# The third batch's q and v are loaded during the second pass of an attention and MLP kernel

## The chip, the cores and the metric

The kernel runs on one core of a Trainium2 chip. The metric is device time in microseconds of one execution of the whole program. The program before takes 803.91 us, the median of nine runs from 802.67 to 804.8. A profiled execution gives the trace that all views below come from.

## The reference

Attention with grouped heads over 8 batches of 384 positions, 16 query heads, 4 key and value heads, head size 64; then a ResMLP block over the 1024 columns that the heads make together:

```python
scores = (q @ k^T) / sqrt(64)                  # each k, v head serves 4 q heads
x      = softmax(scores) @ v                   # 8 x 384 x 1024
u      = x + lam * (w_tok @ (alpha1 * x + beta1))
out    = u + lam * (relu((alpha2 * u + beta2) @ w_ch1) @ w_ch2)   # 1024 -> 4096 -> 1024
```

Inputs and output are float32; the kernel computes its matrix products from bf16 operands.

## The kernel before

**Passes.** After an opening part that computes the attention of the first batch, `main(b)` runs once for each of the 8 batches. A pass has two stages on the tensor engine (TensorE, PE). The *W1 stage* computes `h = relu(a2 @ w_ch1)` in 16 chunks of 256 hidden columns (L414): a chunk is two groups of 8 matmuls 128x384. The *W2 stage* computes `h @ w_ch2` in 6 output tiles of 32 matmuls 128x512 (L447). `w_ch2` stays in SBUF from the first pass on; `w_ch1` does not fit beside it and is loaded anew in each pass, chunk by chunk.

**Attention of the next batch rides along.** `main` yields at points of both stages, four times in each chunk of the W1 stage (units 0 to 63), and the loop at the end of the kernel calls there what a table has for that unit. `side(b + 1)` gives two tables, one for each stage. In the W2 stage of pass b go scores, exp, products with v and token mixing of batch b + 1. In the W1 stage go only its preparations: for the second pass, `turns` in `side(2)` has `q_transpose` at units 16, 24 and 32, six 128x128 transposes on TensorE into a PSUM bank each (L203), and a copy to `qT` by DVE (L205). Each handles two of the eight head pairs; so pairs 2 to 7 of the third batch are turned in chunks 4, 6 and 8.

**Batches and passes.** The index of a batch counts from 0. "Third batch" is b = 2, and its attention is prepared in the second pass (b = 1).

**Loads of weights and inputs.** POOL issues the loads that cast from float32 to bf16, and they all go through one queue in the order of the program: W1 chunks (`load_w1`, L134), w2 (`load_w2`, L139), q (`load_q`, L116, four loads of four heads, 192 KB each) and v (`load_v`, L111, three of 64 KB). W1 has a ring of RING = 5 buffers. In `main`, after chunk c, `load_w1` issues the load of the chunk five further on; the issue waits on POOL until chunk c has been read, and whatever stands behind it on POOL waits with it. At the end of the W1 stage of the first pass POOL issues the first five chunks of the second pass and then calls `load_next(2)`: `place_k` (four copies of k on POOL), q and v of the third batch.

**SP.** SP issues k's loads (L96), the stores of the output (L454) and DMA transposes: a2 for the next pass (L297), k (`flip_k`, L119) and, where the table `moves` says so, q (`flip_q`, L123). For b == 1, `moves` has `flip_k` and `flip_q` for pairs 0 and 1 of the third batch, at unit 1 of the W1 stage. SP's instructions run in order; behind those two come the k loads for the fourth batch.

From the third pass on, q of the next batch is loaded and flipped by DMA during W2 stages; the change does not touch this.

Of the kernel before, what the change touches and what calls it, by code (L numbers as in the profile page):

```python
# [12 lines left out]
def kernel(  # L13
# [23 lines left out]
    bf = mybir.dt.bfloat16  # L37
# [6 lines left out]
    B, Hq, S, D = q.shape  # L44
    Hkv = k.shape[1]
    G = Hq // Hkv
    DM = Hq * D
    DFF = moe_w_ch1.shape[1]
    P = 128
    NST = S // P  # L50
# [6 lines left out]
    NCH = NNT // CW  # L57
    RING = 5
# [5 lines left out]
    sb = ST(tc.tile_pool(name="sb", bufs=2))  # L64
# [22 lines left out]
    def by_st(ap):  # L87
        return ap.rearrange("h (p st) d -> p st h d", st=NST)

    ks, k2s, qrs = {}, {}, {}  # L90
# [8 lines left out]
    def place_k(b, i, hs=(0, 1)):  # L99
        if b not in k2s:  # L100
            k2s[b] = sb.tile([P, NST, Hkv, 2, D], bf, tag="k2", name="k2", bufs=1)
        copies = [nc.gpsimd.tensor_copy] * 2
        if b == 1 or b == 0 == i:
            copies = (nc.vector.tensor_copy, nc.vector.tensor_copy if i else nc.scalar.copy)
        lo, hi = hs[0], hs[-1] + 1
        for a in range(2):
            copies[a](out=k2s[b][:, :, 2 * i + lo:2 * i + hi, a, :], in_=ks[b][i][:, lo:hi].rearrange("p h st d -> p st h d"))

    def load_v(b, sts=range(NST)):
        for st in sts:  # L110
            nc.gpsimd.dma_start(out=vt[b % 2][:, st, :, :D], in_=by_st(v[b])[:, st])  # L111

    def load_q(b):
        qrs[b] = sb.tile([P, Hq, NST, D], bf, tag="q_raw", name="q_raw", bufs=1)
        for h in range(0, Hq, G):
            nc.gpsimd.dma_start(out=qrs[b][:, h:h + G], in_=q[b, h:h + G].rearrange("h (p st) d -> p h st d", st=NST))  # L116

    def flip_k(b):
# [11 lines left out]
    def load_w1(n):  # L130
        if n < B * NCH:
            t = sb.tile([P, NDT, CW * P], bf, tag="w1", name="w1", bufs=RING)
            c = n % NCH
            nc.gpsimd.dma_start(out=t, in_=w1src[:, :, c * CW * P:(c + 1) * CW * P])  # L134
            w1_tiles[n] = t

    def load_w2(dw, i, n):
        r, cs = slice(i * NNT // n, (i + 1) * NNT // n), slice(dw * 512, (dw + 1) * 512)
        nc.gpsimd.dma_start(out=w2[:, r, cs], in_=w2src[:, r, cs])  # L139

    def bank(shape, tag, name, dtype=f32):
        if tag == "three":
            return threes[0].tile(shape, dtype, tag="sc", name=name, bufs=3)
        if tag == "mm":
            return mms.tile(shape, dtype, tag="mm", name=name, bufs=2)
        return psum.tile(shape, dtype, tag=tag, name=name, bufs=2 if tag == "sc" else 1)
# [9 lines left out]
    def evac(eng):  # L156
        return nc.scalar.copy if eng == "ACT" else nc.vector.tensor_copy
# [16 lines left out]
    def side(b):  # L174
# [177 lines left out]
        if not first:  # L352


            turns = {16 + 8 * i: [(q_transpose, 2 + 2 * i, 2, "three")] for i in range(3)} if b == 2 else {}
            if b == 1:
                turns = {4: [(split, 2, 4, 0)], 8: [(split, 2, 4, 1)], 12: [(k_transpose, 0)],
                         16: [(q_transpose, 0, 2, "av")], 20: [(k_transpose, 2)]}
                for i in range(3):
                    turns[24 + 4 * i] = [(q_transpose, 2 + 2 * i, 2, "av")]  # L360
                for i in range(4):
                    turns[34 + 4 * i] = [(spread, (2 * i, 2 * i + 1), (1, 3), "tp", "ACT")]
                for i in range(2):
                    turns[50 + 4 * i] = [(spread, range(4 * i, 4 * i + 4), (3, 4), "av", "ACT")]
            return turns, {
                0: [(scores3, 0)], 4: [(av, 0)], 6: [(scores3, 1)], 8: [(tok_flip, 0)], 11: [(av, 1)],
                13: [(scores3, 2, True)], 15: [(av, 2)], 16: [(tok_flip, 1)], 18: [(tok_flip, 2)], 19: [(av, 3)],
                21: [(scores3, 3)], 23: [(tok_flip, 3)], 25: [(av, 4)], 27: [(scores3, 4)], 29: [(tok_flip, 4)],
                31: [(av, 5)], 33: [(scores3, 5, True)], 35: [(av, 6), (tok_flip, 5)], 37: [(av, 7)],
                39: [(tok_flip, 6)], 41: [(tok_flip, 7)]}  # L370
# [25 lines left out]
    def load_next(b):  # L396
        place_k(b, 0)
        place_k(b, 1)
        load_q(b)
        load_v(b)  # L400


    def main(b):
        a2T = a2Ts[b % 2]
        x = xs.pop(b)
        n = S + 1 if b == 0 else S
        for c in range(NCH):
            w1 = w1_tiles.pop(b * NCH + c)
            for j in range(CW):
                nt = c * CW + j  # L410
                begun = b == 0 and nt in early
                ps = early[nt] if begun else bank([P, 512], "mm", "h")
                for dt in range(0 if begun else NDT):
                    nc.tensor.matmul(out=ps[:, :n], lhsT=w1[:, dt, j * P:(j + 1) * P],  # L414
                                     rhs=a2T[:, dt, :n], start=(dt == 0), stop=(dt == NDT - 1))
                    if dt == 3:
                        yield 0
                c1 = bias1[:, nt:nt + 1]
                if b == 0:
                    evac("DVE" if nt % 2 else "ACT")(out=c1, in_=ps[:, S:n])  # L420
                if nt % 2 == 0:
                    nc.scalar.activation(out=hT[:, nt, :], in_=ps[:, :S], func=RELU, bias=c1)  # L422
                else:
                    nc.vector.tensor_scalar(out=hT[:, nt, :], in0=ps[:, :S], scalar1=c1,  # L424
                                            scalar2=0.0, op0=ADD, op1=mybir.AluOpType.max)
                yield 0

            if b or c + RING < NCH:
                load_w1(b * NCH + c + RING)
            if b == 0 and c == NCH - RING:  # L430
                for i in range(3, 8):
                    load_w2(0, i, 8)
                for i in range(8):
                    load_w2(1, i, 8)
            if b == 0 and c == NCH - 1:
                for i in range(RING):
                    load_w1(NCH + i)
                load_next(2)
        for dw in range(NDW):
            cs = slice(dw * 512, (dw + 1) * 512)  # L440
            for ms in range(NST):
                ps = bank([P, 512], "mm", "ch")
                o = sb.tile([P, 512], f32, tag="tmp", name="o", bufs=4)
                last = (b, dw, ms) == (B - 1, NDW - 1, NST - 1)
                for lo, hi in ((0, 256), (256, 384), (384, 512)) if last else ((0, 512),):
                    for nt in range(NNT):
                        nc.tensor.matmul(out=ps[:, lo:hi], lhsT=hT[:, nt, ms * P:(ms + 1) * P],  # L447
                                         rhs=w2[:, nt, dw * 512 + lo:dw * 512 + hi], start=(nt == 0), stop=(nt == NNT - 1))
                        if nt % 4 == 3 and nt < NNT - 1:
                            yield 1  # L450
                    c = slice(dw * 512 + lo, dw * 512 + hi)
                    nc.vector.tensor_tensor(out=o[:, lo:hi], in0=ps[:, lo:hi], in1=lam_t[:, c], op=MUL)  # L452
                    nc.vector.tensor_tensor(out=o[:, lo:hi], in0=o[:, lo:hi], in1=x[:, ms, c], op=ADD)  # L453
                    nc.sync.dma_start(out=out[b].rearrange("(p st) d -> p st d", st=NST)[:, ms, c], in_=o[:, lo:hi])  # L454
                yield 1
# [3 lines left out]
    with tc.manual_schedule(engines=order):  # L459
# [110 lines left out]
        load_k(2)  # L570
        for b in range(B):
            us = side(b + 1) if b + 1 < B else ({}, {})
            moves = [(0, 1, flip_k, 2), (0, 1, flip_q, 2, 0, 2)] if b == 1 else []
            if 0 < b < B - 2:
                moves += [(1, 1, load_k, b + 2), (1, 2, load_next, b + 2), (1, 34, flip_k, b + 2), (1, 36, flip_q, b + 2, 0, 2),
                          (1, 37, flip_q, b + 2, 2, 2), (1, 42, flip_q, b + 2, 4, 2), (1, 43, flip_q, b + 2, 6, 2)]
            for i, u, *m in moves:
                us[i].setdefault(u, []).append(m)
            done = [0, 0]
            for second in main(b):  # L580
                if b == second - done[1] - 1 == 0:
                    lead_banks.close()
                    threes.append(ST(tc.psum_pool(name="threes", bufs=3)))
                for f, *a in us[second].get(done[second], []):
                    f(*a)
                done[second] += 1
# [28 lines left out]
```

The softmax here doesn't subtract the row's maximum and nothing guards it: scores larger than these inputs give would overflow.

## Time and profile before

| what | value |
|---|---|
| median of nine runs | 803.91 us |
| profiled execution | 804.8 us, of which span of the trace 803.0 us |
| TensorE busy | 794.8 us, 99% of the span |
| granted clock of TensorE | 0.999 of full |
| second pass, W1 stage | 133.0 to 176.8 us |
| third pass, W1 stage | 232.0 to 273.6 us |
| W1 loads issued on POOL (L134) | 128 of 512 KB, 0.87 us of POOL each |
| W1 loads issued 134 to 180 us, issue to landing | 9.5 / 10.5 / 10.8 us (least, median, most) |
| W1 loads issued 232 to 276 us, issue to landing | 6.3 / 8.2 / 9.5 us |

The page of a profile shows busy time of each engine, the span in 40 slices, the DMA queues, the chain that ended last, and the costliest groups of instructions. Times in the views are in us from the start of the span. In a timeline each line has start, duration, engine, line of the kernel, operation, what is written and read, count, and in brackets how long the engine stood idle before it and who ended that. PEld is TensorE's weight load, which runs beside its matmuls. An idle time of a loading engine such as POOL means that it waited for a buffer, and costs nothing in itself. "Landing" is the time from a DMA's issue to its completion. The DMA share in a table of windows counts the packets' time in all queues against 16 engines, and can exceed 1.

### The profile page before, as it was taken

How to read it: one execution, taken by the hardware profiler on the slowest of the kernel's cores; microseconds unless marked ns; L12 is line 12 of the kernel's file. 1: busy time of each engine (PE TensorE's matmuls, PEld its weight loads, DVE VectorE, ACT ScalarE, POOL GpSimd, SP SyncE). 2: the span in 40 equal slices, each digit the busy share in tenths (PEclk: the TensorE clock that was granted, in tenths of full speed). 3: DMA queues.
4: the chain of work that ended last, by engine and by line, in shares of the span. 5: the costliest groups of instructions: out<-in, count | busy, mean ns of one | idle time of the engine just before them, and what ended most of it. 6: DMA issues, size and time to landing. Idle time of an engine off the chain costs nothing.

```text
span 803.0 us, 14253 instructions
## 1 busy us (share of the span) xinstructions
PE 794.8 (99%) x6141; PEld 453.3 (56%) x6141; DVE 344.2 (43%) x667; ACT 226.5 (28%) x308; POOL 182.0 (23%) x241
## 2 busy tenths in 40 slices
PE   8999999999999999999999999999999999999997
PEld 4766555655556555565555655566555655556545
DVE  7652555225552256323662236622365225552122
ACT  7624331223402233123221233122431223312100
POOL 9234231342013500135002340033300330003000
PEclk9999999999999999999999999999999999999999
DMA  9999999999269962999439991499914994139611
GB/s 189 202 194 202 202 207 160 190 198 134 65 132 187 198 95 62 160 189 196 74 80 156 198 195 45 95 175 198 160 47 113 169 198 86 47 64 179 88 40 40
DMA packets 232575, 112.58 MB, mean 140 GB/s; under 512 B 81976, under 2 KB 226368, under 8 KB 232512
## 3 DMA queue, kind: packets, MB, share of 16 engines
q0 software_dynamic: 170752, 83.47, 78.8%
q1 hardware_dynamic: 61216, 27.81, 14.0%
q8 instruction: 48, 0.79, 0.4%
q10 hardware_dynamic: 544, 0.39, 0.1%
q14 instruction: 15, 0.12, 0.1%
HBM read 170.53 MB, written 12.58 MB: 228 GB/s over the span
## 4 chain that ended last, share of the span: by engine, by line
PE 85%; DMA 9%; issue 3%; DVE 1%; POOL 1%; SPq 0%; ACT 0%; POOLq 0%; DVEq 0%
PE ch L447 37%; PE h L414 36%; DMA w<-in_moe_w_ch_dram 9%; PE sc L217 4%; PE sc L252 3%; PE sc L275 3%; POOL w L134 1%; PE h L168 1%; DMA hT<-in_moe_lam_dram 1%; PE tok L275 0%; PE av L252 0%; PE ut L292 0%; DVE x L258 0%; PE tp L203 0%; DVE hT L532 0%
## 5 line engine op out<-in xcount | busy, mean ns | idle before, releaser
L447 PE MATMUL ch<-w,hT 128*128 128x512 bf16 (+2 forms) x1600 | 357.6, 371 | 0.9 <-DVE o L452 0.9
L414 PE MATMUL h<-a2T,w 128*128 128x384 bf16 (+1 forms) x2016 | 332.1, 326 | 0.6 <-DMA w<-in_moe_w_ch_dram 0.6
L414 PEld LDWEIGHTS <-w 128*128 128x128 bf16 x2016 | 196.2, 98 | 131.2 <-DMA w<-in_moe_w_ch_dram 2.7
L134 POOL DMA_DIRECT2D w<-in_moe_w_ch_dram x128 | 112.2, 877 | 527.8 <-PE h L414 507.5
L447 PEld LDWEIGHTS <-hT 128*128 128x128 bf16 x1600 | 144.7, 98 | 152.6 <-issue 10.1
L226 ACT ACTIVATE es<-sc 128x1024 bf16<-128x1024 f32 x126 | 121.4, 1023 | 187.7 <-PE sc L217 178.8
L424 DVE TENSOR_SCALAR hT<-h,bias 128x384 bf16<-128x384 f32 x128 | 79.1, 618 | 216.0 <-PE h L414 215.4
L422 ACT ACTIVATE hT<-h,bias 128x384 bf16<-128x384 f32 x128 | 74.3, 580 | 305.0 <-PE h L414 304.4
L452 DVE TENSOR_TENSOR o<-ch,vecs 128x512 f32<-128x512 f32 (+2 forms) x50 | 33.5, 669 | 108.8 <-PE ch L447 108.8
L252 PEld LDWEIGHTS <-es 128*128 128x128 bf16 x1008 | 38.2, 97 | 13.2
L275 PEld LDWEIGHTS <-wtokT 128*128 128x128 bf16 x576 | 37.4, 98 | 12.3 <-DVE a L265 1.7
L217 PE MATMUL sc<-qT,kT 64*128 64x384 bf16 (+2 forms) x576 | 41.9, 271 | 0.2
L252 PE MATMUL sc<-v,es 128*128 128x65 bf16 x1008 | 39.8, 193 | 0.0
L257 DVE RECIPROCAL rinv<-sc 128x6 f32<-128x6 f32 x56 | 10.8, 193 | 67.2 <-PE sc L252 66.4
L282 DVE TENSOR_TENSOR x<-sc,x 128x384 f32<-128x384 f32 x56 | 31.0, 553 | 20.0 <-PE sc L275 20.0
L275 PE MATMUL sc<-a,wtokT 128*128 128x128 bf16 x504 | 37.3, 219 | 0.0
L217 PEld LDWEIGHTS <-kT 64*128 64x128 bf16 x576 | 21.7, 94 | 24.0 <-issue 19.0
L453 DVE TENSOR_TENSOR o<-o,x 128x512 f32<-128x512 f32 (+2 forms) x50 | 33.5, 671 | 1.7
L286 DVE TENSOR_TENSOR a<-x,vecs 128x384 bf16<-128x384 f32 x56 | 31.8, 567 | 1.9
L263 DVE TENSOR_TENSOR a1f<-x,vecs 128x384 f32<-128x384 f32 x56 | 31.2, 558 | 1.9
L265 DVE TENSOR_TENSOR a<-a1f,vecs 128x384 bf16<-128x384 f32 x56 | 31.2, 558 | 1.9
L258 DVE TENSOR_TENSOR x<-sc,rinv 128x384 f32<-128x384 f32 x56 | 31.2, 558 | 1.9
(80 smaller groups left out, 212.0 us busy)
## 6 DMA issues: line engine op xcount, KB each, us to landing
w<-in_moe_w_ch_dram POOLq DMA_DIRECT2D x144, 512.0 KB, 9.0
out_dram<-o SPq DMA_DIRECT2D x47, 256.0 KB, 2.1
q_raw<-in_q_dram POOLq DMA_DIRECT2D x28, 192.0 KB, 8.8
kst<-in_k_dram SPq DMA_DIRECT2D x16, 192.0 KB, 6.2
v<-in_v_dram POOLq DMA_DIRECT2D x24, 64.0 KB, 8.7
a2T<-a SPq DMA_TRANSPOSE x56, 2.3
qg<-in_q_dram POOLq DMA_DIRECT2D x3, 192.0 KB, 5.8
stage<-in_q_dram ACTq DMA_DIRECT2D x2, 192.0 KB, 3.7
```

What stands on the lines that cost most here:

```text
L134: nc.gpsimd.dma_start(out=t, in_=w1src[:, :, c * CW * P:(c + 1) * CW * P])
L217: nc.tensor.matmul(out=sc[:, hh, k % 4:k % 4 + n], lhsT=kT[r, sk, 2 * p // G, :], rhs=qT[r, p, st:st + n, :], start=True, stop=True)
L226: nc.scalar.activation(out=e, in_=sc, func=EXP, scale=scale_qk)
L252: nc.tensor.matmul(out=av[:, hh, sq, :], lhsT=ess[k // 4][:, m % 2, k % 4, :], rhs=vb[:, sk, hk, :], start=(sk == 0), stop=(sk == NST - 1))
L275: nc.tensor.matmul(out=ps[:, tt, :], lhsT=wtokT[:, st, tt * P:(tt + 1) * P], rhs=a1s[p][:, st, :], start=(st == 0), stop=(st == NST - 1 an ...
L286: nc.vector.tensor_tensor(out=a2s[p], in0=u, in1=bc(al2, p), op=MUL)
L414: nc.tensor.matmul(out=ps[:, :n], lhsT=w1[:, dt, j * P:(j + 1) * P], rhs=a2T[:, dt, :n], start=(dt == 0), stop=(dt == NDT - 1))
L422: nc.scalar.activation(out=hT[:, nt, :], in_=ps[:, :S], func=RELU, bias=c1)
L424: nc.vector.tensor_scalar(out=hT[:, nt, :], in0=ps[:, :S], scalar1=c1, scalar2=0.0, op0=ADD, op1=mybir.AluOpType.max)
L447: nc.tensor.matmul(out=ps[:, lo:hi], lhsT=hT[:, nt, ms * P:(ms + 1) * P], rhs=w2[:, nt, dw * 512 + lo:dw * 512 + hi], start=(nt == 0), sto ...
L452: nc.vector.tensor_tensor(out=o[:, lo:hi], in0=ps[:, lo:hi], in1=lam_t[:, c], op=MUL)
L453: nc.vector.tensor_tensor(out=o[:, lo:hi], in0=o[:, lo:hi], in1=x[:, ms, c], op=ADD)
```

## The change

For the third batch only: `load_next(2)` at the end of the first pass's W1 stage is replaced by its `place_k` calls. q's four loads are issued one by one in the second pass, after the W1 loads that follow chunks 1, 2, 3 and 4. v's three loads are issued after the W1 load that follows chunk 11. The DMA transpose of pairs 0 and 1 on SP is taken away, and TensorE turns all four groups of q, at units 24, 32, 40 and 48 (chunks 6, 8, 10, 12).

```diff
-    def load_q(b):
-        qrs[b] = sb.tile([P, Hq, NST, D], bf, tag="q_raw", name="q_raw", bufs=1)
-        for h in range(0, Hq, G):
+    def load_q(b, hs=range(0, Hq, G)):
+        if b not in qrs:
+            qrs[b] = sb.tile([P, Hq, NST, D], bf, tag="q_raw", name="q_raw", bufs=1)
+        for h in hs:
             nc.gpsimd.dma_start(out=qrs[b][:, h:h + G], in_=q[b, h:h + G].rearrange("h (p st) d -> p h st d", st=NST))
...
-            turns = {16 + 8 * i: [(q_transpose, 2 + 2 * i, 2, "three")] for i in range(3)} if b == 2 else {}
+            turns = {24 + 8 * i: [(q_transpose, 2 * i, 2, "three")] for i in range(4)} if b == 2 else {}
...
             if b == 0 and c == NCH - 1:
                 for i in range(RING):
                     load_w1(NCH + i)
-                load_next(2)
+                place_k(2, 0)
+                place_k(2, 1)
+            if b == 1 and c in range(1, 5):
+                load_q(2, [G * (c - 1)])
+            if b == 1 and c == NCH - RING:
+                load_v(2)
...
-            moves = [(0, 1, flip_k, 2), (0, 1, flip_q, 2, 0, 2)] if b == 1 else []
+            moves = [(0, 1, flip_k, 2)] if b == 1 else []
```

## The prediction

> **What bounds the kernel now.** I read the page first: TensorE is busy 794.8 of 803.0 us at full granted clock in all 40 slices, so a change can only lose or win where TensorE waits. Then I compared the W1 stage of the second pass (the one that the change touches) with that of the third and fourth, in a table of windows: length of the window, busy time of each engine, and at the end granted clock, DMA share, GB/s.
>
> ```profile
> 133.00:177.00 44.00, 43.40 (x276) 25.66 (x275) 12.34 (x21) 9.28 (x16) 13.12 (x15) 1.00 1.32 180
> 232.00:273.60 41.60, 41.60 (x257) 25.05 (x256) 10.65 (x17) 9.30 (x16) 13.12 (x15) 1.00 1.34 189
> 328.64:370.25 41.61, 41.61 (x257) 24.96 (x256) 10.65 (x17) 9.28 (x16) 13.12 (x15) 1.00 1.33 188
> ```
>
> An undisturbed W1 stage lasts 41.6 us, 2.60 a chunk. The second pass's lasts from 133.02 to 176.8, 43.8. Of the 2.2 us more, three turns of q on TensorE are 3 x 0.34 = 1.0 (the third batch's pairs 2 to 7), and 1.2 is waiting for W1. The timeline of weight loads shows where:
>
> ```profile
> 149.33 0.44 PEld L414 LDWEIGHTS <-w 128*128 128x128 bf16 x4 [0.60 <-DMA w<-in_moe_w_ch_dram]
> ...
> 163.56 2.39 PEld L414 LDWEIGHTS <-w 128*128 128x128 bf16 x16 [0.77 <-DMA w<-in_moe_w_ch_dram]
> 166.25 2.39 PEld L414 LDWEIGHTS <-w 128*128 128x128 bf16 x16 [0.30 <-DMA w<-in_moe_w_ch_dram]
> 168.88 2.39 PEld L414 LDWEIGHTS <-w 128*128 128x128 bf16 x16 [0.25 <-DMA w<-in_moe_w_ch_dram]
> 171.52 2.39 PEld L414 LDWEIGHTS <-w 128*128 128x128 bf16 x16 [0.24 <-DMA w<-in_moe_w_ch_dram]
> 174.17 2.39 PEld L414 LDWEIGHTS <-w 128*128 128x128 bf16 x16 [0.27 <-DMA w<-in_moe_w_ch_dram]
> ```
>
> From chunk 11 on each chunk starts 2.64 us after the last, at the pace of its load and not of its 16 matmuls. So the end of this stage is set by the DMA queue. The windows around it say when that queue had room:
>
> ```profile
> 125.00:132.00 7.00, 7.00 (x48) 3.71 (x46) 4.05 (x8) 0.00 (x0) 0.00 (x0) 1.00 1.62 185
> 132.00:136.00 4.00, 4.00 (x25) 2.25 (x24) 1.57 (x3) 0.58 (x1) 0.00 (x0) 1.00 0.19 59
> 136.00:144.00 8.00, 8.00 (x51) 4.83 (x50) 2.05 (x4) 1.74 (x3) 2.75 (x4) 1.00 1.24 136
> 144.00:177.00 33.00, 32.40 (x209) 19.01 (x208) 8.72 (x16) 6.96 (x12) 10.37 (x12) 1.00 1.44 201
> ```
>
> Full until 132, nearly empty to 136, disturbed to 144 (136 GB/s), then full at about 198 GB/s to the end of the stage. The POOL timeline says whose loads these are:
>
> ```profile
> 99.84 0.88 POOL L134 DMA_DIRECT2D w<-in_moe_w_ch_dram x1 [2.99 <-DVE a L265]
> 100.71 2.19 POOL L107 CAST k<-kst 128x384 bf16<-128x384 f32 x4
> 102.86 0.76 POOL L116 DMA_DIRECT2D q_raw<-in_q_dram  x1
> ...
> 122.80 0.74 POOL L111 DMA_DIRECT2D v<-in_v_dram  x1 [3.38 <-DMA w<-in_moe_w_ch_dram]
> 136.08 0.88 POOL L134 DMA_DIRECT2D w<-in_moe_w_ch_dram  x1 [12.54 <-PE h L414]
> ```
>
> The list of DMA issues, cut to one issue at a time, gives landings. Chunk 4, issued at 99.84, lands at 125.1. The third batch's q lands behind it at 126.5, 127.3, 128.4 and 130.2, its v by 131.5. Chunk 5 can be issued only at 136.08, when chunk 0 gives up its buffer. So today q and v travel while nobody waits for the queue.
>
> **The change, part by part.**
>
> *q and v leave 102.9 to 131.5.* Gain: nothing. They are behind chunks 0 to 4 in the same queue, so those land no earlier; the matmuls from 78 to 133 show no wait; chunk 0 starts at 133.02 because the W2 stage ends then. The hole in the queue grows from 4 to about 11 us and stays unused, since chunk 5 still needs chunk 0's buffer.
>
> *q, four loads of 192 KB, behind chunks 6, 7, 8 and 9.* On POOL each issue takes 0.74 us, beside 0.87 for W1, in a period of 2.6: no cost. In the queue, consecutive q loads of a later batch land at 188.5, 189.4, 190.4, 191.4: 1.05 us each once they follow one another. All four lie ahead of chunk 10 in a queue that sets the stage's end: 4 x 1.05 = +4.2 us. What could hide it is the hole at 132 to 136, but they are issued from about 139.6 on. The rows alone would allow a smaller cost only if q ran in gaps, and from 144 on there are none (201 GB/s).
>
> *One DMA transpose of q gone from SP (pairs 0 and 1, issued at 136.67 behind k's).* This is the disputed term. Below: its data phase when nothing else runs, seen in the fine DMA rows at 224 to 232, is 0.93 us (196 KB at about 211 GB/s). Above: from 136 to 144 the queues moved 136 GB/s where 198 would do, which is 8 x 62 = 0.5 MB or 2.5 us lost, and with its own 1.0 that is 3.5 if all of the loss were its doing; part of it is not, as the first chunk of the third and fourth pass starts slowly too. Nearest row: landings counted from the first packet of the first chunk issued in the stage. In the third pass (no transposes then) the second and third chunk land 8.7 and 11.3 us after it; in the second pass, from 138.2, 11.1 and 13.7. The difference is 2.4; the second pass carries in that time also the two k loads (2 x 192 KB, about 2 us), which in the third lie ahead of the first packet, but which will now move at 138 to 140, while the first chunk runs slowly in any case. I leave 0.5 for them: -1.9 us. The two k loads on SP, queued behind the transpose, go out 1.6 us earlier and cost the same bytes.
>
> The Trainium skill, "Advanced Engine Details and Errata", X-Bar Transpose (TRN2), says that transposing DMAs are as fast as plain ones. Alone this one is, in the trace; beside W1 its packets are spread over 139.9 to 144.6, with 1 us at 141.5 in which hardly anything moves. By the rule the term would be its bytes, -1.0, and the sum +3.2. "DMA: Bandwidth & Descriptors", Specifications, wants 512 B per transfer for full rate; a q row in SBUF has 384 B. The trace has q at 188 GB/s against 198 for W1, so the loss is 5% here, and it is in the 1.05.
>
> *Four turns of q on TensorE instead of three, at chunks 6, 8, 10, 12 instead of 4, 6, 8.* One more turn is 0.34 us of TensorE and a DVE copy of 0.56; DVE is busy 12.3 of 44 us. On a stage paced by loads the turn lies inside the waits. A turn needs its q: the first, 0.65 us into chunk 6 (149.3), with q landing near 148.5, has 0.8 us to spare. If q were later, chunk 7's weights are behind it in the same queue, so this wait replaces one that would come anyway.
>
> *v behind chunk 11's issue.* Its queue place is behind the next pass's chunk 0, which lands near 179; three loads of 0.5 us land by 181. The first product with v comes 5.3 us into the W2 stage (182.1 now, 184.6 then). Cost nothing, 3 us of cover. Its 1.5 us of queue delay only chunks of the third pass, which have 50 us.
>
> **The sum, walked chunk by chunk.** New landing = old landing - 1.9 + 1.05 for each q load ahead. Old landings of chunks 6 to 15: 149.3, 151.9, 154.6, 157.2, 159.9, 163.5, 166.2, 168.9, 171.5, 174.2. New: 147.4, 151.0, 154.8, 158.5, 162.2, 165.9, 168.5, 171.2, 173.8, 176.5. TensorE takes 2.60 a chunk, 2.94 with a turn, and starts at the later of its own end and the landing: chunk 6 at 148.6, then 151.6, 154.8, 158.5, 162.2, 165.9, 168.5, 171.4, 174.0, 176.6, end 179.2. Against 176.8: **+2.4 us**. Everything behind it moves by the same. With the transpose at -0.9 the same walk ends at 180.1 (+3.3); at -3.5, near 177.6 (+0.8), because TensorE's own turns then set part of it.
>
> The profiled execution took 804.8 us (span 803.0 and 1.8 around), so it would become 807.2; the median of the nine runs, 803.91, is 0.9 below it, and there I forecast 803.9 + 2.4 = **806.3**.
>
> **Rivals.** About 0.2%, 1.6 us, is what a measurement here can tell from no change.
>
> 1. *The transpose was the trouble* (ends at no change). If removing it gives back most of what was lost between 136 and 144, from 2.6 us on the sum falls under 1.6: 804.7 to 805.4. For it: 1 us of near standstill at 141.5, in its middle. Against: the slow start of the first chunk in passes without it. Chance 0.22.
> 2. *Only bytes count* (slower by more). The transpose gives back 0.9 to 1.0, q costs 4.2, and first turns wait too: +3.2 to +4.2, 807.1 to 808.1. For: its own 0.93 us alone. Chance 0.25.
> 3. *The loads hide* (the change does not do what it costs): q travels in TensorE's slack, all waits of the stage go, and one turn comes on top: -1.2 + 0.34 = -0.9, 803.0. It needs a queue with room after 144; it has none. Even this lies within 0.2%. Chance 0.04, with 0.03 more for a gain that I do not see.
> 4. *v late*: if the queue runs 3 us later than walked, the W2 stage of the second pass stops at its first product with v. Then +1 to +3 on top, 807.3 to 809.3. Chance 0.04.
>
> The forecast itself has 0.42, at +1.6 to +3.2. Slower by over 0.2%: 0.42 + 0.25 + 0.04 = 0.71. Within: 0.22 + 0.04 = 0.26. Faster: 0.03. The range goes from 804.3 (the sum at its lower end, +0.8, less 0.4 for the spread of medians) to 808.1 (rival 2's upper end); it leaves out rival 3 and most of 4.
>
> **What would show it.** In the changed profile, the W1 stage of the second pass should start at 133.0 and end near 179; waits for W1 should come at chunks 8, 9, 10 and 11, of 0.6 to 1.1 us each, where now there are 0.2 to 0.4; DMA should be nearly idle from about 126 to 135; after the q loads the chunks again follow at 2.64; all later passes keep 96.6 us. Chunk 6 should land near 147.4; at 148.4 rival 2 is right, under 146.8 rival 1. I am wrong if the stage ends before 178, or if time is lost in another stage.

## The result, and the profile after

The changed kernel takes 806.26 us (median of 10 runs, 805.26 to 807.25) against 803.87 before (30 runs): a ratio of 1.0033, with an interval from 1.0025 to 1.0041. It is slower by 2.4 us.

Line numbers in the changed kernel are higher by 1 to 6 (L414 becomes L415, L134 becomes L135, L203 becomes L204). The windows of before, asked of the changed kernel's trace:

```profile
125.00:132.00 7.00, 7.00 (x41) 3.45 (x40) 3.01 (x6) 0.00 (x0) 0.00 (x0) 1.00 0.24 67
132.00:136.00 4.00, 4.00 (x26) 2.39 (x25) 2.00 (x3) 0.58 (x1) 0.88 (x1) 1.00 0.39 102
136.00:144.00 8.00, 8.00 (x52) 4.83 (x50) 1.85 (x3) 1.90 (x4) 4.45 (x6) 1.00 1.19 185
144.00:177.00 33.00, 30.54 (x201) 18.21 (x200) 9.03 (x15) 6.30 (x12) 13.08 (x16) 1.00 1.50 195
```

From 125 to 132 the queues now move 67 GB/s instead of 185: the hole is wider and nobody fills it. From 136 to 144 they move 185 instead of 136: without q's transpose the disturbed stretch is nearly gone. From 144 on they are full as before, and TensorE is busy for 30.5 of 33 us instead of 32.4. (The second pass begins 1.08 us earlier in this profile, at 131.94. In windows moved by that much the rates are 83, 45, 187 and 196 GB/s: the reading is the same.) The weight loads of the second pass's W1 stage show where:

```profile
148.47 1.78 PEld L415 LDWEIGHTS <-w 128*128 128x128 bf16 x12
150.62 2.39 PEld L415 LDWEIGHTS <-w 128*128 128x128 bf16 x16 [0.37 <-DMA w<-in_moe_w_ch_dram]
154.35 0.44 PEld L415 LDWEIGHTS <-w 128*128 128x128 bf16 x4 [1.34 <-DMA w<-in_moe_w_ch_dram]
...
158.00 2.39 PEld L415 LDWEIGHTS <-w 128*128 128x128 bf16 x16 [0.93 <-DMA w<-in_moe_w_ch_dram]
161.74 0.44 PEld L415 LDWEIGHTS <-w 128*128 128x128 bf16 x4 [1.34 <-DMA w<-in_moe_w_ch_dram]
...
162.68 5.03 PEld L415 LDWEIGHTS <-w 128*128 128x128 bf16 x32
...
168.22 9.58 PEld L415 LDWEIGHTS <-w 128*128 128x128 bf16 x60
```

The waits are at chunks 8, 9 and 10 (the starts at 154.35, 158.00 and 161.74), each behind one q load more than the chunk before; at chunk 7 there is next to none, and from chunk 11 on none. TensorE's own idle time there is 0.95 + 0.55 + 0.96 = 2.5 us. From the start of chunk 10, 29.8 us into the stage, TensorE sets the pace and not the queue: six chunks and two turns, 6 x 2.60 + 2 x 0.34 = 16.3 us, end the stage at 46.1. POOL's timeline shows the loads behind which the chunks wait, here the first two of the four:

```profile
138.06 0.88 POOL L135 DMA_DIRECT2D w<-in_moe_w_ch_dram  x1 [2.17 <-PE h L415]
138.93 0.76 POOL L117 DMA_DIRECT2D q_raw<-in_q_dram  x1
140.21 0.88 POOL L135 DMA_DIRECT2D w<-in_moe_w_ch_dram  x1 [0.52 <-PE h L415]
141.08 0.76 POOL L117 DMA_DIRECT2D q_raw<-in_q_dram  x1
```

Cut into stages by TensorE's timeline (first matmul of a stage to first matmul of the next), the two profiles agree everywhere but in two places. The second pass's W1 stage lasts 46.08 us instead of 43.77: +2.31, the whole of the result. And the opening of the profiled execution before was 1.28 us longer: the first matmul with W1 begins at 28.77 there and at 27.49 here. The change touches nothing of it; the opening differs from run to run. So the profiled times (804.8 and 806.16) differ by less than the medians do. All other stages agree within 0.2 us: W2 stages 55.05, the third W1 stage 41.60, everything from the second W2 stage's end to the last matmul 567.8.

### The profile page after: what moved, and what is told of

It reads as the page before. It is cut to its first block, busy times and chain, and to the rows that moved or that the text cites. A ratio compares the mean times of both kernels' runs of the same rounds, so it can differ in the third digit from the quotient of the medians.

```text
span 804.3 us, 14264 instructions
## 1 busy us (share of the span) xinstructions
PE 795.0 (99%) x6147; PEld 453.8 (56%) x6147; DVE 343.8 (43%) x668; ACT 226.3 (28%) x308; POOL 182.5 (23%) x241
## 4 chain that ended last, share of the span: by engine, by line
PE 96%; DMA 2%; DVE 1%; ACT 1%; issue 0%; POOL 0%; POOLq 0%
PE ch L453 42%; PE h L415 39%; PE sc L218 4%; PE sc L253 4%; PE sc L276 3%; DMA w<-in_moe_w_ch_dram 2%; PE h L169 1%; ACT hT L227 1%; PE tok L276 0%; PE av L253 0%; PE warm L470 0%; PE tp L204 0%; PE ut L293 0%; PE vec L333 0%; PE tok L280 0%
## 5 line engine op out<-in xcount | busy, mean ns | idle before, releaser
L415 PE MATMUL h<-a2T,w 128*128 128x384 bf16 (+1 forms) x2016 | 332.6, 326 | 2.5 <-DMA w<-in_moe_w_ch_dram 2.5
L415 PEld LDWEIGHTS <-w 128*128 128x128 bf16 x2016 | 196.4, 98 | 133.0 <-DMA w<-in_moe_w_ch_dram 4.4
L135 POOL DMA_DIRECT2D w<-in_moe_w_ch_dram x128 | 112.3, 878 | 542.6 <-PE h L415 520.7
L218 PEld LDWEIGHTS <-kT 64*128 64x128 bf16 x576 | 21.8, 94 | 24.3 <-issue 18.5
```

Of the source, the lines that this page charges most:

```text
L218: nc.tensor.matmul(out=sc[:, hh, k % 4:k % 4 + n], lhsT=kT[r, sk, 2 * p // G, :], rhs=qT[r, p, st:st + n, :], start=True, stop=True)
```

## The experiments

The theory: in the second pass's W1 stage a full DMA queue sets the pace, each q load ahead of a W1 chunk costs its 1.05 us, and taking q's DMA transpose out of that stage gives about 1.9 us back. Rivals: the turns on TensorE or the lateness of q or v cost, or the transpose is worth only its bytes. Each kernel's ratio is against runs of the kernel before on the same chip, where the median of before was 803.49 to 803.87; "stage" is the second pass's W1 stage in its one profile.

| kernel | median us | ratio, interval | stage us |
|---|---|---|---|
| before | 803.87 | | 43.77 |
| changed | 806.26 | 1.0033, 1.0025 to 1.0041 | 46.08 |
| q and v early, four turns | 803.43 | 0.9997, 0.9988 to 1.0006 | 43.38 |
| three q late, transpose kept | 807.14 | 1.0039, 1.0026 to 1.0053 | 46.62 |
| three q late, turn instead | 805.50 | 1.0021, 1.0012 to 1.0029 | 44.69 |
| changed, v early | 806.54 | 1.0036, 1.0023 to 1.0049 | 45.74 |
| changed, k late | 806.48 | 1.0034, 1.0021 to 1.0046 | 46.94 |
| before, k late | 803.28 | 0.9992, 0.9983 to 1.0001 | 43.16 |
| transposes in the first pass | 806.08 | 1.0026, 1.0017 to 1.0035 | 44.67 |
| changed, each q twice | 810.44 | 1.0092, 1.0076 to 1.0108 | 52.04 |
| before, k and v late | 802.61 | 0.9991, 0.9981 to 1.0000 | 42.60 |
| changed, q early | 802.81 | 0.9995, 0.9986 to 1.0003 | 42.94 |
| k and v late, two transposes | 803.84 | 1.0005, 0.9997 to 1.0014 | 43.89 |

**q and v back in the first pass.** In the changed kernel:

```diff
-                place_k(2, 0)
-                place_k(2, 1)
-            if b == 1 and c in range(1, 5):
-                load_q(2, [G * (c - 1)])
-            if b == 1 and c == NCH - RING:
-                load_v(2)
+                load_next(2)
```

> The changed kernel, but with q and v of the third batch loaded at the end of the first pass's W1 stage as before; still four turns on TensorE at chunks 6 to 12 and no DMA transpose of q. Theory (q's bytes in a full queue cost, the transpose gone gives back): no load of q stands ahead of a W1 chunk, all waits for W1 go, the second pass's W1 stage lasts 16 x 2.60 + 4 x 0.34 = 43.0 us, 803.1 us in all (-0.8 against before, -3.2 against the changed kernel). Rival (the later and additional turns on TensorE cost, not the loads): about 806. Rival (POOL's issues between W1 issues cost, not the bytes): 803.1 too, told apart by the run with the q loads left between but fewer.

The four turns are still there, at the same chunks, and the loss is gone: the rival of the turns falls. No wait for W1 is left, but the stage is 43.38 and not 43.0. Two gaps of 0.3 us in the weight loads appear in its first chunk, and the last transpose of a2 lands 5.1 us after its issue; in the changed kernel it takes 2.3, in the profile before 3.5. With q and v in the queue at that time, a2 for the second pass comes just late.

**Only q back, v stays late.** The same edit, but `load_q(2)` in place of `load_next(2)` and v's lines kept.

> The changed kernel with only q's four loads put back into the first pass; v stays behind chunk 11, four turns on TensorE, no DMA transpose of q. Theory: no q ahead of a W1 chunk, and fewer bytes beside the last transposes of a2: W1 stage 43.0 us, -0.6 to -0.8 against before, about 3 less than the changed kernel. Rival (q early alone still holds up a2's last transposes): as the run with q and v early, within 0.2 of before.

That gap goes too (a2's last transpose 3.1 us), and the stage is 42.94, the forecast's 41.6 + 4 x 0.34. The rest of the timeline of weight loads has no wait at all:

```profile
148.26 5.03 PEld L415 LDWEIGHTS <-w 128*128 128x128 bf16 x32
153.35 0.48 PEld L204 LDWEIGHTS <-q_raw 128*128 128x128 bf16 x6
153.79 5.03 PEld L415 LDWEIGHTS <-w 128*128 128x128 bf16 x32
158.89 0.48 PEld L204 LDWEIGHTS <-q_raw 128*128 128x128 bf16 x6
159.33 5.03 PEld L415 LDWEIGHTS <-w 128*128 128x128 bf16 x32
```

Against the changed kernel only the place of q's four loads differs. So their lateness costs 46.08 - 42.94 = 3.1 us here. In the queue they cost more: chunk 10 lands 29.75 us after the start of the stage with them and 25.42 without, 4.33 later, or 1.08 for each load. The difference is slack: without them the weights of chunk 10 are there 1.3 us before TensorE wants them. The other rival, that POOL's issues cost and not the bytes, fails in the changed kernel's own trace: its W1 loads of this stage land 8.9 to 13.7 us after their issue, while the queue moves 195 GB/s, so the queue always had loads waiting.

**Each q load twice.** In the changed kernel, behind each `load_q`:

```diff
+                again = sb.tile([P, G, NST, D], bf, tag="es", name="again", bufs=EB)
+                nc.gpsimd.dma_start(out=again, in_=q[2, G * (c - 1):G * c].rearrange("h (p st) d -> p h st d", st=NST))
```

> The changed kernel with each of the four q loads between the W1 loads issued a second time into a spare buffer that nobody reads: 8 loads of 192 KB instead of 4. Theory (1.05 us of full queue each): +4.2 on top of the changed kernel, 810.0 to 810.6. Rival (the lateness of q for its turns is what costs): little more, under 807.

810.44, 4.2 more than the changed kernel: four more loads of 1.05. The trace shows it without the spread of the medians: chunk 10 lands 34.05 us into the stage, 4.30 later than in the changed kernel. The profiled execution took 813.0; its waits are at chunks 7 to 10, each 0.9 to 1.2 longer than in the changed kernel:

```profile
152.58 2.39 PEld L415 LDWEIGHTS <-w 128*128 128x128 bf16 x16 [1.61 <-DMA w<-in_moe_w_ch_dram]
157.25 0.44 PEld L415 LDWEIGHTS <-w 128*128 128x128 bf16 x4 [2.28 <-DMA w<-in_moe_w_ch_dram]
...
161.98 2.39 PEld L415 LDWEIGHTS <-w 128*128 128x128 bf16 x16 [2.00 <-DMA w<-in_moe_w_ch_dram]
166.75 0.44 PEld L415 LDWEIGHTS <-w 128*128 128x128 bf16 x4 [2.38 <-DMA w<-in_moe_w_ch_dram]
```

The stage, 52.04 us, can't be compared as it is, because in this execution the granted clock of TensorE fell to one half, right after the fourth wait; the number before the DMA share in a window is that clock:

```profile
167.36:170.78 3.42, 3.42 (x17) 1.95 (x15) 0.56 (x1) 0.58 (x1) 0.00 (x0) 0.50 1.46 198
```

Half of 3.42 us is 1.7. Without it the stage would be about 50.3 (an estimate), 4.3 longer than the changed kernel's. TensorE had been idle for 1.23, 1.90, 1.62 and 2.00 us within 17 us. No profile with shorter waits has such a stretch, but one profile does not show which wait brought it on.

**The transpose by itself.** Two kernels with three q loads late and the first early; the first keeps `flip_q` for pairs 0 and 1 and drops that turn, the second is as the changed kernel:

```diff
-            if b == 1 and c in range(1, 5):
+            if b == 1 and c in range(2, 5):
...
                 place_k(2, 0)
                 place_k(2, 1)
+                load_q(2, [0])
...
-            moves = [(0, 1, flip_k, 2)] if b == 1 else []
+            moves = [(0, 1, flip_k, 2), (0, 1, flip_q, 2, 0, 2)] if b == 1 else []
```

(the last two lines in the first of them alone, with turns for i in range(1, 4)).

> The first of the four q loads goes back to the first pass and its DMA transpose back to SP; the other three stay between the W1 loads, with three turns at chunks 8, 10 and 12. Theory: three loads of 1.05 in the full queue and the transpose's cost kept: +2.5 to +3.3 against before, 806.4 to 807.2, although one q load fewer is late than in the changed kernel. Rival (only bytes count, transpose worth 1.0): 806.4 to 807.2 as well; it is the difference to the next run that tells them apart.

> As the run before, three q loads between the W1 loads, but the first q group is turned by TensorE at chunk 6 in place of the DMA transpose. The difference to the run before is the transpose alone (and a turn of 0.34 us, inside the waits). Theory (transpose worth 1.9 us of queue): +0.9 to +1.4 against before, 804.8 to 805.3, which is 1.4 to 2.0 less than the run before. Rival (only bytes count, 1.0 us): +1.7 to +2.3, 805.6 to 806.2, 0.8 to 1.0 less than the run before.

The difference is 1.93 us by the stages and 1.6 by the medians: the transpose is worth nearly 2 us, not 1.0. It rests on the stages. They are 2.85 and 0.92 longer than before's, both within the theory's ranges. The medians lie 3.65 and 2.0 above those of before on the same chip, higher than the theory's +3.3 and +1.4 at most, and the second lies within the rival's +1.7 to +2.3; the executions of each kernel spread over 1.2 us and more, so the medians alone would not decide. The DMA rows from 138 to 144 us (40 slices of 0.15 us) show one half of it. First with the transpose, then without:

```profile
DMA  0396767489999999999940010999999999999999
GB/s 0 41 102 79 61 48 58 48 63 101 133 172 283 172 166 171 152 142 73 44 12 7 10 10 10 154 191 189 172 183 191 181 181 179 186 186 181 181 190 235
```

```profile
DMA  4799999999999999999999999999999999999999
GB/s 49 65 104 157 273 167 174 169 167 191 188 237 230 230 229 232 234 246 232 242 234 242 219 219 217 210 201 188 205 195 188 205 198 198 195 205 195 198 191 208
```

About 1 us with hardly any bytes (the 12, 7, 10, 10, 10), and the transpose's own 0.2 MB is another. The stop, 0.8 to 1.1 us long, is in all five profiles that have this transpose in the W1 stage (before included, at 141.5), directly behind a 16 KB instruction fetch, and in none of those without it, which have the fetch too.

**v alone back.** `load_v(2)` behind `place_k` again.

> The changed kernel with v alone loaded early as before. Theory: v stands behind all W1 chunks that the second pass needs, so it costs nothing: within 0.3 us of the changed kernel, 806.0 to 806.5. Rival (v late holds up the W2 stage or the later W1 loads): 805.3 or less.

Same within the measurement. In the changed kernel v lands by 179.1 and its first product starts at 183.2 without a wait.

**The fourth batch's k loads out of the way.** In both kernels, `load_k` and `load_next` of the fourth batch at units 8 and 9 of the second pass's W2 stage instead of 1 and 2, so that on SP the k loads stand behind an output store there.

> The changed kernel, with the fourth batch's k loads (two of 192 KB on SP) and what depends on them moved from the start of the second pass to its W2 stage, behind the first output store, where the queues are empty. Theory (any bytes that share the queue between 136 us and the end of the W1 stage push the W1 chunks back): 0.4 MB less, 1.5 to 2.0 us, so 804.5 to 805.0. Rival (only what POOL puts between the W1 loads counts, SP's queue does not): unchanged, 806.3.

> The kernel before with only the same move of the fourth batch's k loads to the W2 stage. Theory: the 1.2 us of waits for W1 in the second pass go, the three turns stay: -1.0 to -1.2, 802.7 to 802.9. Rival (the DMA transposes alone make the waits): at most -0.2, 803.7.

In the kernel before all waits for W1 go; what is left of the 43.16 beyond 42.62 are the same gaps in the first chunk as with q and v early (a2's last transpose 5.3 us). In the changed kernel nothing is won (its stage is even 0.86 longer, 46.94), and the theory in its simple form, that any bytes in the stage push W1 back, is wrong there. Windows of the changed kernel with k late, and then of the changed kernel:

```profile
137.00:141.00 4.00, 4.00 (x27) 2.45 (x25) 1.23 (x2) 0.58 (x1) 2.40 (x3) 1.00 1.16 146
141.00:147.00 6.00, 6.00 (x39) 3.60 (x38) 1.23 (x2) 1.69 (x3) 4.08 (x6) 1.00 1.36 164
```

```profile
137.00:141.00 4.00, 4.00 (x26) 2.43 (x25) 1.23 (x2) 0.58 (x1) 2.42 (x3) 1.00 1.04 161
141.00:147.00 6.00, 6.00 (x39) 3.62 (x37) 1.23 (x2) 1.72 (x3) 4.07 (x6) 1.00 1.45 201
```

Without k's 0.4 MB the queues moved 1.57 MB from 137 to 147 us, with it 1.85: most of the room was left empty, at 164 GB/s, and chunk 6 landed at 146.9 in both. Why the W1 loads ran below 198 GB/s there (the third pass's first loads do so too, at 163 to 189 from 238 to 246) stays open.

**All transposes by DMA in the first pass.** From the kernel before: no turns for b == 2, `flip_k` at unit 34 of the first pass's W2 stage, four `flip_q` at unit 43.

> The kernel before, with q and v early, but k and all four groups of q turned by DMA in the first pass's W2 stage: k at unit 34, q behind the last transposes of a2, when the POOL queue runs empty (131 to 136 us); no turns on TensorE. Theory: 4 x 0.93 us of transposes use the hole, the second pass's W1 stage has neither turns nor transposes of k ahead of its loads: 41.6 to 42.2 us against 43.8, so -1.6 to -2.2, 801.7 to 802.3. Rival (the transposes run into the first chunks of the second pass and hold up its W1 loads as now): 803.5 or more.

Wrong: slower by 2.2 us by the medians, and the stage is 0.9 longer. All waits for W1 and all turns are gone as expected, but k's transpose goes into the full queue at 117, q lands at 129.3 to 135.6 and v by 138.3 (before: 126.4 to 130.1, and 131.5), and the last transposes of a2 land late (7.6 and 7.8 us after their issue). TensorE stands in the first chunk:

```profile
131.56 1.14 PE L414 MATMUL h<-a2T,w 128*128 128x384 bf16 x6
134.28 0.32 PE L414 MATMUL h<-a2T,w 128*128 128x384 bf16 x1 [1.59 <-DMA a2T<-a]
135.77 4.55 PE L414 MATMUL h<-a2T,w 128*128 128x384 bf16 x27 [1.17 <-DMA a2T<-a]
```

The hole from 132 to 136 is no longer there to be used: the queues move 147 GB/s in it, where before they moved 59. The stage accounts for only part of the 2.2 us. The profiled execution took 804.06 us at a granted clock of 1.000, and so did two others (803.9 and 804.2); the other eight had a mean clock of 0.996 to 0.998 and took 805.7 to 807.1. The run with each q load twice had a mean of 0.998 with its 3.42 us at half clock, and the same here would explain most of the rest; but none of the eight was profiled, so it is not shown.

**Towards a better kernel.** From the kernel before, with k and v late as above; the second kernel has `flip_q` for pairs 2 and 3 as well and two turns.

> The kernel before with the fourth batch's k loads in the second pass's W2 stage (as in the run that moved only those) and the third batch's v behind chunk 11 (as in the changed kernel); q stays early. Theory (q and v early do cost: up to 0.5 us, because the last transposes of a2 land late beside them; k loads make the waits for W1): W1 stage of the second pass 41.6 + 3 x 0.34 = 42.6 us against 43.8, so -1.0 to -1.2 against before. Rival (what is saved at its start comes back as waits for W1): no better than the run with k moved alone, -0.4.

> As the first kernel of this call (k and v late, q early), with a second DMA transpose of q (pairs 2 and 3) behind the first, and two turns on TensorE instead of three. Theory (one transpose holds the W1 queue up by 1.9 us; with k's 0.4 MB gone there is about 2 us of room): no or small waits, W1 stage 42.3 to 42.9, -0.9 to -1.4 against before. Rival (there is no room): waits of 1 to 2 us come, 43.5 or more, 0 or slower.

The first has no wait in the stage: 42.60, as worked out. 802.61 is the lowest median of all, 0.9 below its own runs of before, but the interval ends at 1.0000: as a gain it is at the edge of what is measured. A second transpose brings the waits back (chunks from 11 on again 2.64 apart, 43.89): there was no room for it.

## Why the prediction was right, point by point

**The sum** was +2.4; the medians give +2.4 and the stage +2.3. **The place** was right: the second pass's W1 stage alone, with waits at chunks 8, 9 and 10 of about the size forecast. That the sum fits so closely is in part luck: chunk 10 started 29.8 us into the stage where the walk had 29.2, and chunk 11 had no wait where the walk had about 0.7. The two misses, both from the course of the transpose below, cancel.

**q's loads.** 1.05 us each in a full queue: shown by doubling them (chunk 10 lands 4.30 later) and by taking them away (4.33 earlier, of which TensorE gains 3.1 because 1.3 us of slack comes in between). The landings from which the prediction read the 1.05, as it gives them, are 0.97 apart; in the trace they are 188.47, 189.48, 190.52 and 191.60, 1.04 apart, so the term was right.

**The transpose.** Its 1.9 us were right as a total and wrong in their course. Landings from the start of the stage:

| chunk | before | forecast | after |
|---|---|---|---|
| 6 | 16.3 | 14.4 | 15.0 |
| 8 | 21.5 | 21.8 | 22.4 |
| 10 | 26.9 | 29.2 | 29.8 |
| 11 | 30.5 | 32.9 | 32.4 |
| 15 | 41.1 | 43.5 | 43.0 |

Up to chunk 10 removing it gave 1.3, from chunk 11 on 2.3: the kernel before has a gap of 3.61 us between the landings of chunks 10 and 11, where others are 2.6 to 2.7, and the walk carried it over. It went with the transpose. The other four kernels that keep the transpose in this stage have such a gap as well, 3.5 to 3.7 us at chunk 11 or 12, and the kernels without it have none there.

The trace shows where the gap comes from. Each load ends with 16 packets of 4 bytes, and it lands with the last of them. In the kernel before, the 16 of chunk 10 come within half a microsecond, between 159 and 160. Of chunk 11's, 15 come by 162.3 and the last one at 163.2 (packets "under 512 B" from 161.5 to 162.3, then from 162.3 to 163.3):

```profile
DMA packets 306, 0.15 MB, mean 186 GB/s; under 512 B 15, under 2 KB 306, under 8 KB 306
DMA packets 389, 0.20 MB, mean 199 GB/s; under 512 B 1, under 2 KB 389, under 8 KB 389
```

To the end of the stage one packet stays 1 us behind in this way. Chunk 11's are the first behind the stage's second instruction fetch, one packet of 16 KB that takes 0.95 us at 160.9. In the changed kernel one packet is 1.6 us behind the middle ones from chunk 5 on, and the second fetch adds nothing. The other ten profiles of these two kinds (all but the one with every transpose in the first pass) go the same way: with the transpose in the stage, the 16 packets lie within 0.2 to 0.6 us of the middle ones behind the stop, and the last falls 1.0 to 1.6 us behind at the second fetch; without it, the last is 1.0 to 1.6 us behind all along. By the middle packets of chunk 10, then, the removal had given 2.6 us already; the late packet hid half of it until, from chunk 11 on, the kernel before had one too. That a late packet is one DMA engine held up is likely but not shown, as the trace does not name the engine of a packet. What makes it late from chunk 5 on in the changed kernel, and why everything stops beside a transpose, stays open.

So rival 1 held part of the truth, that more than bytes was lost. Rival 2, bytes alone, fits the landings up to chunk 10 (chunk 6 came 0.6 us later than forecast, where 1.0 was its sign), but not the stages of the pair of experiments, which differ by 1.93. The Trainium skill's "Advanced Engine Details and Errata", X-Bar Transpose (TRN2), has transposes as fast as plain DMAs; beside W1 loads 196 KB cost 1.9 us of the stage here, and 0.93 alone. The prediction's "alone this one is" compared its 211 GB/s with W1's 198. The k loads, plain transfers on SP, move 305 GB/s at 235.5 to 236.5 of the same trace, so against those the transpose is slower alone, too.

**"Gain: nothing" for q and v leaving the first pass** held against the profile before. The experiments limit it: with q and v early the last transposes of a2 land after 3.5 to 5.3 us, and in two of the profiles TensorE lost 0.4 to 0.5 us to that.

**v late** cost nothing, as said. Its cover was 4.1 us (landing 179.1, use 183.2), forecast 3. **The turns** were not free: the prediction had them inside waits, but behind the last wait, at chunk 10, nothing waits any more, and the turns in chunks 10 and 12 lengthen the stage by 2 x 0.34 = 0.7 us. In the kernel before, its last turn, in chunk 8, lay ahead of the wait at chunk 11.

**The profiled execution** was forecast at 807.2 and took 806.16, because the one before had an opening 1.28 us longer; the forecast on the median was not touched by that.

## What to carry to other kernels

Before a load is moved, ask whether its new place is a queue whose pace somebody already waits for: there it pushes what stands behind it back by its whole transfer time (4.3 us here), and the reader loses that less its own slack (3.1 us here), and in its old place it may have been free because the queue ran dry later anyway. A busy share does not show this; the spacing of the consumer's starts (2.64 against 2.60 us) does. Read a small change stage by stage: the third pass's W1 stage lasts 41.6 us in all thirteen profiles, while the opening alone varies by more than 1 us.

## What the runs showed of the hardware that was not expected

A DMA transpose of 196 KB runs at about 211 GB/s by itself, but alternates with W1 packets when both are in flight, and in five of five such profiles both queues stopped for about 1 us behind an instruction fetch of 16 KB. Each load ends with 16 packets of 4 bytes, and it lands with the last: with the queue full and the 16 close together, an instruction fetch left one of them about 1 us behind for the rest of the stage, in five of five profiles. A full queue of W1 loads moves 198 GB/s, but the first loads after an idle stretch do not: in the changed kernel with k late 164 GB/s over 6 us, with several loads already issued. In one execution with four waits of TensorE of 1.2 to 2.0 us within 17 us, the granted clock was 0.50 for the next 3.4 us.
